# Attention by straight and cross halves in a chain of linear attention and two feed-forward layers

## Chip, cores and metric

One core of one Trainium2 chip runs the whole program. The time is device microseconds from launch to end, as the median of three runs, and lower is better.

## The reference, cut to what matters

Attention is a decayed linear recurrence: for each of 4 batches and 8 heads a 64x64 state is multiplied by the head's decay and takes the outer product of k and v at each of 768 positions, and q reads it. Two feed-forward layers follow (512 to 1024 to 512 with a softmax gate and a layer norm, then 512 to 2048 to 512 with h cos h).

```python
gamma = 1.0 - 2.0 ** (-5.0 - np.arange(H))
for t in range(S):
    state = gamma[None, :, None, None] * state + np.einsum('bhd,bhe->bhde', k[:, :, t], v[:, :, t])
    y[:, :, t] = scale * np.einsum('bhd,bhde->bhe', q[:, :, t], state)
```

```python
h = x @ w_in
e = np.exp(h - np.max(h, axis=-1, keepdims=True))
solu = h * e / (np.sum(e, axis=-1, keepdims=True) + 1e-09)
ln = (solu - mu) / np.sqrt(var + 1e-06) * g_ln
x = ln @ w_out          # second layer: (h * np.cos(h)) @ w_out
```

The weights arrive as 64-bit floats and are turned into 32-bit ones on the chip.

## The kernel before, in words

**Attention steps.** The sequence is cut into 12 chunks of 64 positions; two batches go together, so there are 24 steps (`steps`, line 80), and a step holds 8 heads of two batches: 16 blocks of 64x64. A partition half of 64 rows holds the even heads, the other the odd ones; `j` counts the 8 column blocks. A step n has three batches of matmuls. *Scores* (`score_pair`, line 225): q times k of the chunk, into the PSUM tile `sc`; the operands lie in the other half from the output, so they use the cross corners of the array. *State* (`state_pair`, line 233): k times v of the chunk, accumulated over the chunks into the PSUM tile `S`, in the straight corners. *Outputs* (`att_out`, line 282): one matmul per block over all 128 rows. For that, tile `W` holds v in one half and the state before the chunk in the other, and tile `X` holds the masked scores in the one half and q in the other, so that one product of 128 rows adds both contributions, into the PSUM tile `y`.

**Around the matmuls.** `score_mask` (line 244) is two products on VectorE of 64 partitions each, by a table `mg` of mask and decay that GpSimd scales for each step (`att_prep`, line 216). `att_prep` also scales k by its decay, in four ScalarE operations (line 223). `state_copy` (line 253) is two ScalarE copies of 64 partitions, which move the state to the other half. The output product with the second part of `mg` (line 290) makes `x32`, the rows that the first layer takes. `load_step` (line 83) issues six loads per step on SP's queue: kt, q in two halves, v in two halves, kn; a step's tiles are reused three steps later (`kt`: two).

**Order.** TensorE's order is the program's, written out by hand. The other engines' queues are filled by a planner that simulates a timeline, so an operation can be queued there ahead of its place in the program. Each engine's queue runs in its order. Lines 489 to 518 write out the first steps; from then on `attend` (line 457) is called between the pieces of the first layer: up to line 533 once per half block of rows, then in the loop from line 537 once or twice per round. While weights are still read two at a time (before line 536) scores, state and outputs are three batches; after it scores of step n+1 and state of step n alternate, and the outputs of step n follow.

**What else runs there.** `load_w` (line 142) turns a weight tile into 32-bit floats in one ScalarE operation and four VectorE operations (lines 158 to 168). `norm` (line 318) is the softmax gate and layer norm of 128 rows, with a power on GpSimd (line 334), whose result VectorE (335) and ScalarE (336) wait for. `transp` (line 341) transposes the result, 16 transposes into a PSUM tile that ScalarE and VectorE (line 355) empty. After some 350 us only the second layer is left.

Of the kernel before, what the change touches and what calls it, by code (L numbers as in the profile page):

```python
# [22 lines left out]
C = 64  # L23
# [27 lines left out]
def body(ctx: ExitStack, tc: tile.TileContext, qx, kt, kn, vn, c_sc, c_mg,  # L51
# [31 lines left out]
    def load_step(n):  # L83
        bp, i = steps[n]
        d = {}
        d["kt"] = pa.tile([128, 8, C], F32, tag="kt", name="kt", bufs=2)
        d["X"] = pa.tile([128, 2, 8, C], F32, tag="X", name="X")
        d["kn"] = pa.tile([128, NHP, 2 * D], F32, tag="kn", name="kn")
        d["W"] = pa.tile([128, 2, 8, D], F32, tag="W", name="W")
        d["mg"] = pa.tile([128, 2, NHP, C], F32, tag="mg", name="mg", bufs=2)  # L90
        nc.sync.dma_start(out=d["kt"], in_=kt[bp, i].rearrange("p (j s) -> p j s", s=C))
        src = qx[bp, i].rearrange("p (j s) -> p j s", s=C)
        nc.sync.dma_start(out=d["X"][64:128, 0], in_=src[64:128])
        nc.sync.dma_start(out=d["X"][0:64, 1], in_=src[0:64])
        src = vn[bp, i].rearrange("p (j s) -> p j s", s=D)
        nc.sync.dma_start(out=d["W"][0:64, 0], in_=src[0:64])
        nc.sync.dma_start(out=d["W"][64:128, 1], in_=src[64:128])
# [7 lines left out]
    mg = const.tile([128, 2, NHP, C], F32, name="mg")  # L105
    cs = const.tile([128, 3, NI, NHP], F32, name="cs")
    gcol = const.tile([128, K1], F32, name="gcol")
    nc.scalar.dma_start(out=mg, in_=c_mg.rearrange("p (u a t) -> p u a t", u=2, t=C))
    nc.scalar.dma_start(out=cs, in_=c_sc.rearrange("p (u a t) -> p u a t", u=3, t=NHP))
# [106 lines left out]
    def att_prep(n):  # L216
        bp, i = steps[n]
        d = st[n]
        nc.gpsimd.tensor_tensor(out=d["mg"], in0=mg, in1=cs[:, 0:2, i].unsqueeze(3).to_broadcast([128, 2, NHP, C]),
                                op=ALU.mult)  # L220
        if i + 1 < NI:
            for a in range(NHP):
                nc.scalar.activation(out=d["kn"][:, a], in_=d["kn"][:, a], func=AF.Copy, scale=cs[:, 2, i, a:a + 1])  # L223

    def score_pair(n, j):
        d = st[n]
        if j == 0:
            d["sc"] = psa.tile([128, 8, C], F32, tag="sc", name="sc")
        sc = d["sc"]
        nc.tensor.matmul(out=sc[0:64, j], lhsT=d["kt"][64:128, j], rhs=d["X"][64:128, 0, j], start=True, stop=True)  # L230
        nc.tensor.matmul(out=sc[64:128, j], lhsT=d["kt"][0:64, j], rhs=d["X"][0:64, 1, j], start=True, stop=True)

    def state_pair(n, j):
# [4 lines left out]
        sp = s_ps[0]  # L238
        k3 = d["kn"].rearrange("p a (b d) -> p (a b) d", b=2)
        for r, par in ((slice(0, 64), 0), (slice(64, 128), 1)):  # L240
            nc.tensor.matmul(out=sp[r, j], lhsT=k3[r, j], rhs=d["W"][r, par, j],
                             start=(i == 0 and j == 0), stop=(i == NI - 2 and j == 7), skip_group_check=True)

    def score_mask(n):
        d = st[n]
        sc = d["sc"]
        for r, par in ((slice(0, 64), 0), (slice(64, 128), 1)):
            nc.vector.tensor_tensor(  # L248
                out=d["X"][r, par].rearrange("p (a b) t -> p a b t", b=2),
                in0=sc[r].rearrange("p (a b) t -> p a b t", b=2),  # L250
                in1=d["mg"][r, 0].unsqueeze(2).to_broadcast([64, NHP, 2, C]), op=ALU.mult)

    def state_copy(n):
        nd, sp = st[n + 1], s_ps[0]
        nc.scalar.activation(out=nd["W"][64:128, 0], in_=sp[0:64], func=AF.Copy)
        nc.scalar.activation(out=nd["W"][0:64, 1], in_=sp[64:128], func=AF.Copy)

    def att_scores(n):
        for j in range(8):
            score_pair(n, j)  # L260
        score_mask(n)

    def att_state(n):
        if steps[n][1] + 1 >= NI:
            return
        for j in range(8):
            state_pair(n, j)
        state_copy(n)

    def att_both(n):  # L270
        if steps[n][1] + 1 >= NI:
            att_scores(n + 1)
            return
        for j in range(8):
            score_pair(n + 1, j)
            state_pair(n, j)
        score_mask(n + 1)
        state_copy(n)
# [3 lines left out]
    def att_out(n):  # L282
        d = st[n]
        y = psa.tile([128, 8, C], F32, tag="y", name="y")
        for j in range(8):
            for par in range(2):
                nc.tensor.matmul(out=y[64 * par:64 * par + 64, j], lhsT=d["W"][:, par, j], rhs=d["X"][:, par, j],  # L287
                                 start=True, stop=True)
# [378 lines left out]
```

## Time and profile before

| | before |
|---|---|
| median of 3 runs | 932.8 us (928.63 to 934.05) |
| profiled execution, first to last instruction | 932.8 us |
| TensorE busy | 893.4 us |
| VectorE busy | 622.7 us |
| ScalarE busy | 455.5 us |
| GpSimd busy | 48.0 us |
| granted TensorE clock, mean | 0.985 |

In the profile, PE is TensorE and PEld its weight loads, DVE is VectorE, ACT ScalarE, POOL GpSimd and SP the queue that issues DMAs; a q behind an engine's name is its sequencer. An engine's busy time counts the time in which at least one of its operations runs. PEclk is the granted share of TensorE's full clock. An fp32 matmul is recorded as two passes, so a batch of 16 has 32 records.

### The profile page before, as it was taken

How to read it: one execution, taken by the hardware profiler on the slowest of the kernel's cores; microseconds unless marked ns; L12 is line 12 of the kernel's file. 1: busy time of each engine (PE TensorE's matmuls, PEld its weight loads, DVE VectorE, ACT ScalarE, POOL GpSimd, SP SyncE). 2: the span in 40 equal slices, each digit the busy share in tenths (PEclk: the TensorE clock that was granted, in tenths of full speed). 3: DMA queues.
4: the chain of work that ended last, by engine and by line, in shares of the span. 5: the costliest groups of instructions: out<-in, count | busy, mean ns of one | idle time of the engine just before them, and what ended most of it. 6: DMA issues, size and time to landing. Idle time of an engine off the chain costs nothing.

```text
span 932.8 us, 16044 instructions
## 1 busy us (share of the span) xinstructions
PE 893.4 (96%) x6464; PEld 765.1 (82%) x6464; DVE 622.7 (67%) x1090; ACT 455.5 (49%) x768; POOL 48.0 (5%) x60
## 2 busy tenths in 40 slices
PE   4787999989899999999999999999999999999997
PEld 4676889879799989998888888888888888888886
DVE  6899887587667754566766655756575665656654
ACT  4677666556656555554534333433443343344332
POOL 2112100101011000000000000000000000000000
PEclk7999899989999999999999999999999999999999
DMA  9986354565547422133012002000300030001001
GB/s 260 313 252 194 106 158 146 184 204 161 188 131 226 157 93 90 64 108 111 24 35 56 1 1 73 19 0 1 91 1 1 7 84 1 1 24 45 1 1 46
DMA packets 41884, 85.28 MB, mean 91 GB/s; under 512 B 5457, under 2 KB 11729, under 8 KB 41809
## 3 DMA queue, kind: packets, MB, share of 16 engines
q1 hardware_dynamic: 41376, 83.91, 30.0%
q8 instruction: 51, 0.84, 0.4%
q10 hardware_dynamic: 432, 0.34, 0.1%
q14 instruction: 25, 0.20, 0.1%
HBM read 64.30 MB, written 19.92 MB: 90 GB/s over the span
## 4 chain that ended last, share of the span: by engine, by line
PE 84%; DVE 6%; DMA 5%; ACT 2%; issue 2%; SPq 1%; POOL 0%; DVEq 0%; ACTq 0%
PE h L393 28%; PE acc L418 28%; PE y L368 13%; PE h L315 10%; DMA kn<-kn_dram 3%; PE tr L351 2%; PE y L287 2%; DMA W<-vn_dram 1%; PE sc L230 1%; DVE X L248 1%; DVE wt L164 1%; DVE wt L161 1%; ACT kn L223 1%; ACT junk L328 1%; DVE wt L162 0%
## 5 line engine op out<-in xcount | busy, mean ns | idle before, releaser
L393 PE MATMUL h<-yh,w2h 128*128 128x512 f32 x384 | 149.6, 390 | 0.0
L393 PE MATMUL h<-yl,w2h 128*128 128x512 f32 x384 | 149.4, 389 | 0.0
L393 PE MATMUL h<-yh,w2l 128*128 128x512 f32 x384 | 149.4, 389 | 0.0
L418 PE MATMUL acc<-o2h,gh 128*128 128x512 f32 x384 | 149.4, 389 | 0.0
L418 PE MATMUL acc<-o2h,gl 128*128 128x512 f32 x384 | 149.4, 389 | 0.0
L418 PE MATMUL acc<-o2l,gh 128*128 128x512 f32 x384 | 149.4, 389 | 0.0
L404 ACT ACTIVATE r<-r,hp 128x512 f32<-128x512 f32 x96 | 69.5, 724 | 144.5 <-DVE r L403 144.5
L368 PE MATMUL y<-lth,o1h 128*128 128x256 f32 x384 | 110.2, 287 | 0.0
L368 PE MATMUL y<-ltl,o1h 128*128 128x256 f32 x384 | 108.8, 283 | 0.0
L368 PE MATMUL y<-lth,o1l 128*128 128x256 f32 x384 | 108.6, 283 | 0.0
L401 DVE SCALAR_TENSOR_TENSOR r<-ki,h 128x512 f32<-128x512 int32 x96 | 66.0, 687 | 62.9 <-ACT ki L400 61.9
L405 DVE TENSOR_TENSOR r<-r,h 128x512 f32<-128x512 f32 x96 | 66.0, 687 | 61.6 <-ACT r L404 61.6
L128 DVE TENSOR_TENSOR gl<-r,gh 128x512 fp32r<-128x512 f32 x96 | 66.3, 691 | 45.9 <-ACT gh L125 45.4
L400 ACT ACTIVATE ki<-h 128x512 int32<-128x512 f32 x96 | 57.3, 597 | 74.7 <-PE h L393 74.1
L125 ACT ACTIVATE gh<-r 128x512 fp32r<-128x512 f32 x96 | 60.7, 632 | 65.4 <-DVE r L405 65.4
L393 PEld LDWEIGHTS h<-yh,w2h 128*128 128x128 f32 x384 | 72.1, 188 | 14.9
L418 PEld LDWEIGHTS acc<-o2h,gl 128*128 128x128 f32 x384 | 72.1, 188 | 15.0
L393 PEld LDWEIGHTS h<-yl,w2h 128*128 128x128 f32 x384 | 72.1, 188 | 15.0
L418 PEld LDWEIGHTS acc<-o2l,gh 128*128 128x128 f32 x384 | 72.1, 188 | 14.9
L418 PEld LDWEIGHTS acc<-o2h,gh 128*128 128x128 f32 x384 | 72.0, 188 | 14.9
L393 PEld LDWEIGHTS h<-yh,w2l 128*128 128x128 f32 x384 | 72.1, 188 | 14.8
L315 PE MATMUL h<-w1h,xh 128*128 128x512 f32 x192 | 77.9, 406 | 0.0
(77 smaller groups left out, 1554.3 us busy)
## 6 DMA issues: line engine op xcount, KB each, us to landing
raw<-w_in_dram SPq DMA_DIRECT2D x24, 512.0 KB, 4.4
raw<-w_out_dram SPq DMA_DIRECT2D x24, 512.0 KB, 4.8
kt<-kt_dram SPq DMA_DIRECT2D x24, 256.0 KB, 4.9
X<-qx_dram SPq DMA_DIRECT2D x48, 128.0 KB, 5.0
W<-vn_dram SPq DMA_DIRECT2D x48, 128.0 KB, 4.6
kn<-kn_dram SPq DMA_DIRECT2D x24, 256.0 KB, 5.1
y1d<-ys SPq DMA_DIRECT2D x24, 256.0 KB, 2.1
yt<-y1d SPq DMA_DIRECT2D x24, 256.0 KB, 2.9
```

What stands on the lines that cost most here:

```text
L125: op = nc.scalar.activation(out=hi, in_=src if head is None else head, func=AF.Copy)
L128: nc.vector.tensor_tensor(out=lo, in0=src, in1=hi.bitcast(F32), op=ALU.subtract)
L287: nc.tensor.matmul(out=y[64 * par:64 * par + 64, j], lhsT=d["W"][:, par, j], rhs=d["X"][:, par, j], start=True, stop=True)
L315: nc.tensor.matmul(out=h[:, c], lhsT=a[:, k], rhs=w[:, k, cs], start=(k + m == 0), stop=(k == KD - 1 and m == 2))
L351: nc.tensor.transpose(out=tr[:, e, t * 128:(t + 1) * 128], in_=lns[2 * g + t].rearrange("p c f -> p (c f)")[:, j * 128:(j + 1) * 128], ide ...
L368: nc.tensor.matmul(out=y1[:, e], lhsT=w[:, j, ds], rhs=a[:, j % 2], start=(m == 0), stop=(m == 3 * K1 - 1))
L393: nc.tensor.matmul(out=h, lhsT=w[:, k, cs], rhs=a[:, k], start=(m == 0), stop=(m == 3 * KD - 1))
L400: nc.scalar.activation(out=ki, in_=h, func=AF.Identity, scale=INV2PI, bias=0.25)
L401: nc.vector.scalar_tensor_tensor(out=r, in0=ki, scalar=-C1, in1=h, op0=ALU.mult, op1=ALU.add)
L404: nc.scalar.activation(out=r, in_=r, func=AF.Sin, bias=hp[:, 0:1])
L405: nc.vector.tensor_tensor(out=r, in0=r, in1=h, op=ALU.mult)
L418: nc.tensor.matmul(out=acc, lhsT=a[:, ts_], rhs=w, start=(j == 0 and m == 0), stop=(j == K2 - 1 and m == 2))
```

## The change

Each head stays on one half of the rows. Scores and state are products within a half (the straight corners). The output is no longer one product of 128 rows but two of 64, masked scores times v (`intra`) and state times q, both into the opposite half of `y` (the cross corners), accumulated there. Since scores, state and outputs of a pair of blocks then occupy different corners, `attn` alternates all of them: first scores of step n+1 with the intra products of step n, then state of step n with the state products of step n. v is scaled by its decay instead of k, by GpSimd in place; the mask is a plain triangle from a constant table, applied by one VectorE operation over 128 partitions; the state copy is one ScalarE operation into a tile of its own. k, q, v and k again are laid side by side in DRAM, and a step is loaded by two DMAs of 512 KB. The rows of the first layer's weight are swapped on the host to fit the swapped halves.

```diff
-        nc.sync.dma_start(out=d["kt"], in_=kt[bp, i].rearrange("p (j s) -> p j s", s=C))
-        ...
-        nc.sync.dma_start(out=d["kn"], in_=kn[bp, i].rearrange("p (j s) -> p j s", s=2 * D))
-        if i == 0:
-            nc.gpsimd.memset(d["W"][64:128, 0], 0.0)
-            nc.gpsimd.memset(d["W"][0:64, 1], 0.0)
+        t = pa.tile([128, 4, 8, C], F32, tag="kqvk", name="kqvk")
+        d["kt"], d["q"], d["v"], d["kn"] = (t[:, u] for u in range(4))
+        src = kqvk[bp, i].rearrange("p (u j s) -> p u j s", u=4, s=C)
+        nc.sync.dma_start(out=t[:, 0:2], in_=src[:, 0:2])
+        nc.sync.dma_start(out=t[:, 2:4], in_=src[:, 2:4])
+        d["g"] = pa.tile([128, NHP, C], F32, tag="g", name="g", bufs=2)
+        d["M"] = pa.tile([128, 8, C], F32, tag="M", name="M", bufs=2)
 ...
     def att_prep(n):
-        nc.gpsimd.tensor_tensor(out=d["mg"], in0=mg, in1=cs[:, 0:2, i].unsqueeze(3).to_broadcast([128, 2, NHP, C]),
+        v = d["v"].rearrange("p (a b) e -> p a (b e)", b=2)
+        nc.gpsimd.tensor_tensor(out=v, in0=v, in1=cs[:, 1, i].unsqueeze(2).to_broadcast([128, NHP, 2 * D]), op=ALU.mult)
+        nc.gpsimd.tensor_tensor(out=d["g"], in0=mg[:, 1:], in1=cs[:, 0, i].unsqueeze(2).to_broadcast([128, NHP, C]),
                                 op=ALU.mult)
-        if i + 1 < NI:
-            for a in range(NHP):
-                nc.scalar.activation(out=d["kn"][:, a], in_=d["kn"][:, a], func=AF.Copy, scale=cs[:, 2, i, a:a + 1])
 ...
+    half = (slice(0, 64), slice(64, 128))
     def score_pair(n, j):
+        for r in half:
+            nc.tensor.matmul(out=d["sc"][r, j], lhsT=d["kt"][r, j], rhs=d["q"][r, j], start=True, stop=True)
 ...
+    def out_pair(n, intra, j):
+        l, r = (d["v"], d["M"]) if intra else (d["s"], d["q"])
+        for p in range(2):
+            nc.tensor.matmul(out=d["y"][half[1 - p], j], lhsT=l[half[p], j], rhs=r[half[p], j],
+                             start=(intra and j == 0), stop=(j == 7 and (not intra or steps[n][1] == 0)),
+                             skip_group_check=True)
 ...
     def score_mask(n):
+        nc.vector.tensor_tensor(out=d["M"], in0=d["sc"], in1=mg[:, 0].unsqueeze(1).to_broadcast([128, 8, C]), op=ALU.mult)
     def state_copy(n):
+        s = pa.tile([128, 8, D], F32, tag="s", name="s", bufs=2)
+        nc.scalar.activation(out=s, in_=s_ps[0], func=AF.Copy)
 ...
+    def attn(scores=None, state=None, outs=None):
+        one, two = [], []
+        if scores is not None:
+            one += [(score_pair, scores, j) for j in range(8)]
+        if state is not None and steps[state][1] + 1 < NI:
+            one += [(state_pair, state, j) for j in range(8)]
+        if outs is not None:
+            two += [(out_pair, outs, intra, j) for intra in ((True, False) if steps[outs][1] else (True,)) for j in range(8)]
+        for k in range(max(len(one), len(two))):
+            for q in (one, two):
+                if k < len(q):
+                    q[k][0](*q[k][1:])
+                    if q[k][0] is score_pair and q[k][2] == 7:
+                        score_mask(scores)
 ...
     def attend():
-        if n == 0:
-            att_state(n)
-            att_out(n)
         if n + 1 < ns:
             att_prep(n + 1)
-            if n > 0 and "lt" in p2:
-                att_both(n)
-            else:
-                att_scores(n + 1)
-        if n > 0:
-            if "lt" not in p2:
-                att_state(n)
-            att_out(n)
+        attn(n + 1 if n + 1 < ns else None, n, n)
```

The hand-written first steps (lines 489 to 518) call `attn` for the same batches in the same places.

## Rows read from the trace of the kernel before

**Rows 1.** The page's first part: busy us, share of the span, instructions.

```profile
PE 893.4 (96%) x6464; PEld 765.1 (82%) x6464; DVE 622.7 (67%) x1090; ACT 455.5 (49%) x768; POOL 48.0 (5%) x60
```

**Rows 2.** Stretches: busy us of PE, PEld, DVE, ACT, POOL; PEclk, DMA share, GB/s.

```profile
0.00:27.00 27.00, 14.92 (x231) 13.18 (x232) 14.94 (x26) 13.06 (x27) 5.14 (x13) 0.81 0.96 282
27.00:95.00 68.00, 53.17 (x878) 44.29 (x877) 66.15 (x118) 50.36 (x102) 14.11 (x14) 0.96 0.84 239
95.00:420.00 325.00, 317.30 (x3118) 287.32 (x3118) 224.78 (x438) 189.93 (x315) 28.79 (x34) 0.98 0.46 144
```

**Rows 3.** VectorE's timeline, 23 to 42 us: start us, us, instruction, idle before.

```profile
26.63 0.69 DVE L128 TENSOR_TENSOR w1l<-raw,w1h 128x512 fp32r<-128x512 f32 x1 [2.98 <-ACT w1h L125]
...
38.47 0.69 DVE L290 TENSOR_TENSOR x<-y,mg 128x512 f32<-128x512 f32 x1
39.08 0.68 DVE L167 SCALAR_TENSOR_TENSOR raw<-raw,wt 128x512 int32<-128x512 int32 x1
39.68 1.38 DVE L248 TENSOR_TENSOR X<-sc,mg 64x512 f32<-64x512 f32 x2
41.09 0.69 DVE L167 SCALAR_TENSOR_TENSOR raw<-raw,wt 128x512 int32<-128x512 int32 x1
```

**Rows 4.** VectorE by line, 27 to 95 us: busy us, mean ns, idle.

```profile
L248 DVE TENSOR_TENSOR X<-sc,mg 64x512 f32<-64x512 f32 x18 | 12.3, 684 | 0.2
L167 DVE SCALAR_TENSOR_TENSOR raw<-raw,wt 128x512 int32<-128x512 int32 x11 | 10.1, 919 | 0.1
...
L161 DVE TENSOR_SCALAR wt<-wt 128x512 f32<-128x512 f32 x11 | 6.2, 572 | 0.0
```

**Rows 5.** GpSimd by line, 0 to 420 us.

```profile
L219 POOL TENSOR_TENSOR mg<-mg,cs 128x512 f32<-128x512 f32 x24 | 27.2, 1137 | 210.1 <-DVE x L290 162.0 <-DVE sm L330 45.2 <-DMA cs<-c_sc_dram 2.4
```

**Rows 6.** Three lines of VectorE over the run: duration ns min/median/max.

```profile
L161 DVE TENSOR_SCALAR wt<-wt x48: 414/421/1269, 10.2 to 329.9; 128x512 f32<-128x512 f32 x48
...
L164 DVE SCALAR_TENSOR_TENSOR wt<-raw,wt x48: 674/691/694, 11.1 to 333.0; 128x512 int32<-128x512 int32 x48
...
L167 DVE SCALAR_TENSOR_TENSOR raw<-raw,wt x16: 681/690/1534, 12.1 to 97.1; 128x512 int32<-128x512 int32 x16
```

**Rows 7.** Waits of the run; TensorE's after 93 us: us, times, longest.

```profile
ACT kn L223 <- DMA kn<-kn_dram: 36.0, 16, 5.7
...
PE tr L351 <- DVE ltl L355: 7.6, 5, 4.1
```

**Rows 8.** Two more stretches of the span, columns as in rows 2.

```profile
15.00:20.00 5.00, 2.41 (x32) 2.06 (x32) 5.00 (x9) 1.60 (x4) 1.35 (x1) 0.50 1.06 226
45.00:50.00 5.00, 4.37 (x138) 3.99 (x131) 4.96 (x13) 3.98 (x7) 0.32 (x1) 1.00 1.04 397
```

**Rows 9.** Timeline of TensorE over one attention step in the steady stage.

```profile
220.08 0.22 PE L230 MATMUL sc<-X,kt 64*64 64x64 f32 x1
220.08 0.22 PE L231 MATMUL sc<-X,kt 64*64 64x64 f32 x1
220.09 0.23 PE L241 MATMUL S<-W,kn 64*64 64x64 f32 x2
...
220.89 0.22 PE L230 MATMUL sc<-X,kt 64*64 64x64 f32 x1
...
221.06 1.15 PE L287 MATMUL y<-X,W 128*64 128x64 f32 x32
222.14 0.39 PE L368 MATMUL y<-lth,o1h 128*128 128x256 f32 x1
```

**Rows 10.** The chain of waits, 171 to 192 us: start us, us, what.

```profile
173.33 7.86 DMA kn<-kn_dram
...
181.22 1.28 ACT kn L223 x4
...
183.90 0.56 POOL sm L334
```

**Rows 11.** Landing of the W transfer issued at 175.64 us.

```profile
DMA to landing us min/median/max: 6.7/6.7/6.7
```

More of the change, by code (lines that the diff above doesn't have):

```diff
@@ L50, in body @@
 @with_exitstack
-def body(ctx: ExitStack, tc: tile.TileContext, qx, kt, kn, vn, c_sc, c_mg,
+def body(ctx: ExitStack, tc: tile.TileContext, kqvk, c_sc, c_mg,
          w_in1, w_out1, gln, w_in2, w_out2, out):
@@ L237, in state_pair @@
             s_ps[0] = psa.tile([128, 8, D], F32, tag="S", name="S")
[L238 to L241, printed above, removed]
+        for r in half:
+            nc.tensor.matmul(out=s_ps[0][r, j], lhsT=d["kn"][r, j], rhs=d["v"][r, j],
                              start=(i == 0 and j == 0), stop=(i == NI - 2 and j == 7), skip_group_check=True)
+    def out_pair(n, intra, j):
+        d = st[n]
+        if j == 0 and intra:
+            d["y"] = psa.tile([128, 8, C], F32, tag="y", name="y")
+        l, r = (d["v"], d["M"]) if intra else (d["s"], d["q"])
[3 more added lines that the diff above has]
+                             skip_group_check=True)
@@ new lines, in state_copy @@
+    def state_copy(n):
+        s = pa.tile([128, 8, D], F32, tag="s", name="s", bufs=2)
+        st[n + 1]["s"] = s
+        nc.scalar.activation(out=s, in_=s_ps[0], func=AF.Copy)
[13 more added lines that the diff above has]
+                        score_mask(scores)
+        if state is not None and steps[state][1] + 1 < NI:
+            state_copy(state)
+        if outs is not None:
+            att_out(outs)
@@ L283, in att_out @@
         d = st[n]
[L284 to L288, printed above, removed]
+        y = d["y"]
         x32 = moe.tile([128, NHP, 128], F32, tag="x32", name="x32", bufs=RING)
@@ L495, in body @@
     att_prep(0)
-    att_scores(0)
+    attn(scores=0)
     weights(KD)
-    att_state(0)
-    att_out(0)
+    attn(state=0, outs=0)
     att_prep(1)
-    att_scores(1)
+    attn(scores=1)
     split_x(0)
-    att_state(1)
-    att_out(1)
+    attn(state=1, outs=1)
     mm1(0, 0, [0, 1])
     att_prep(2)
-    att_scores(2)
+    attn(scores=2)
     load_step(3)
@@ L510, in body @@
     mm1(0, 0, [2])
-    att_state(2)
+    attn(state=2)
     mm1(0, 0, [3])
-    att_out(2)
+    attn(outs=2)
     att_prep(3)
-    att_scores(3)
+    attn(scores=3)
     nxt[0] = 3
@@ L612, in _consts @@
     hp = np.arange(NHP)
-    head = 2 * hp[None, :] + (p[:, None] >= 64)
-    gh = gam[head]
-    sl = (p % 64)[:, None, None]
-    mask = np.where(t[None, None, :] >= sl, gh[:, :, None] ** (-1.0 * sl), 0.0)
-    kf = gh[:, None, :] ** (-(64.0 * i[None, :, None] + sl - S / 2))
-    g = gh[:, :, None] ** t[None, None, :] / math.sqrt(D)
-    at = (gh[None] ** (64.0 * i[:, None, None] - S / 2))[..., None]
-    at = at[..., 0]
-    mg = np.stack([mask, g], axis=1).reshape(128, 2 * NHP * C)
-    cs = np.stack([1.0 / at, at, kf.transpose(1, 0, 2)]).transpose(2, 0, 1, 3).reshape(128, 3 * NI * NHP)
+    sl = p % 64
+    par = p // 64
+    gs, gy = (gam[2 * hp[None, :] + m[:, None]] for m in (par, 1 - par))
+    tri = np.where(t[None, :] >= sl[:, None], 1.0, 0.0)[:, None]
+    kf = gs[:, None, :] ** (-(64.0 * i[None, :, None] + sl[:, None, None] - S / 2))
+    g = gy[:, :, None] ** t[None, None, :] / math.sqrt(D)
+    at = gy[:, None, :] ** (64.0 * i[None, :, None] - S / 2)
+    mg = np.concatenate([tri, g], axis=1).reshape(128, (1 + NHP) * C)
+    cs = np.stack([at, kf], axis=1).reshape(128, 2 * NI * NHP)
     return [np.ascontiguousarray(a.astype(np.float32)) for a in (cs, mg)]
```

68 lines of the change are left out of this document (12 added, 56 removed).

## The prediction

> **What bounds the kernel now.** I read the shares first: TensorE is busy nearly the whole span and VectorE two thirds of it [rows 1], but this is an average over stages, so next came the busy times by stretch [rows 2]. The reader is to see three stages there. From 27 to 95 us VectorE is busy 66.15 of 68 us while TensorE has 15 us to spare: VectorE is the bound. From 95 to 420 us TensorE is busy 317.3 of 325 us. After 420 us no attention is left and the change touches nothing. Before 27 us the DMA engines are busy 96% and everything waits for loads. So the first 95 us are to be costed by VectorE and DMA, the stretch from 95 to 350 us by TensorE's own columns and its few waits.
>
> **VectorE: the mask.** Each attention step has two mask products of 64 partitions (lines 248). The timeline shows the slots: the pair that starts at 39.68 lets the next operation start at 41.09, so it takes 1.41 us, and one 128-partition product out of PSUM (L290) takes 39.08 - 38.47 = 0.61 us [rows 3]. The new mask is one operation of that shape: 0.80 us less per step. In the VectorE-bound stage 18 such products stand, nine pairs [rows 4]: 9 x 0.80 = 7.2 us. VectorE hardly idles there, so I count all of it on the path. The floor is 4.0 us, five pairs, if only those after 50 us count because loads hold the others.
>
> **GpSimd: v and g.** Before, GpSimd multiplies 128x512 once per step, 1.137 us [rows 5]. After, it multiplies v (128x512, the same size, so 1.14) and g (half as many columns; by proportion 0.57): 0.57 us more per step, 5.1 us over nine steps. This costs VectorE something. In the same stretch L161 and L167 average 572 and 919 ns [rows 4] where their medians over the run are 421 and 690 [rows 6]: 11 x (151 + 229) = 4.2 us of lengthening, with GpSimd busy 14.11 us [rows 2]. That is 0.30 us per us of GpSimd, so 5.1 us more give 1.5; other operations are lengthened too, so I take 2. Bounds: 0, if the new operations fall beside operations that are not lengthened, and 5.1, if VectorE stands for all of it.
> The Trainium skill, SBUF — State Buffer, "Who interferes with whom", says that a GpSimd operation and a VectorE one that needs their shared port pair exclude each other for a whole instruction, and lists among these VectorE operations with two inputs in SBUF. By that rule alone the 5.1 us would all be lost and the sum would be 3 us higher. The trace agrees only in part: L164 has two SBUF inputs and its longest of 48 is 694 ns against a median of 691 [rows 6].
>
> **ScalarE: four k products and one of two state copies leave.** ScalarE is busy 50.36 of 68 us [rows 2], so its own time costs nothing. What its in-order queue holds up does. Before 26.63 us VectorE stands idle for 2.98 us until ScalarE's w1h arrives [rows 3], and ScalarE waited 36.0 us in 16 places for the DMA of kn [rows 7], one of these just ahead of that w1h. With kn untouched by ScalarE this wait is gone; what is late next is the raw weight's DMA. I take 2.5 of the 2.98 us; bounds 0 and 4, the upper with the loads' gain below.
>
> **DMA.** Six transfers per step (kt, two of X, two of W, kn; rows of 2 KB, four of them on 64 partitions) become two of 512 KB with rows of 4 KB, the form of a raw weight load. Bytes are the same. Where only attention loads land the chip moved 226 GB/s; in a stretch with raw loads, 397 [rows 8]. 1 MB at these rates is 4.6 and 2.6 us, so two steps early in the queue could come 4 us sooner. I don't add this to the 2.5 us, since what VectorE waits for is the ordered work ahead of w1h; it is why I expect no load to take the place of the kn wait. SP issues four transfers fewer per step. Both halves now wait for the end of step n-3's output products, where kt and kn were free earlier by one batch of matmuls.
>
> **TensorE.** Before, a step in the steady stage is 16 groups of four matmuls, one in each quadrant of the array, 0.058 us apart ((220.89 - 220.08) / 14), then 16 pairs of 128-row matmuls from 221.06 to 222.14, 1.08 us [rows 9]. I take 1.09 us for the first batch, the same 16 spacings with a start, so both are 2.17 us. After, 16 straight pairs and 16 cross pairs alternate, in two passes each: 32 groups of four. At the same spacing and one start of 0.16 us (1.08 - 16 x 0.058) that is 2.02 us. Fourteen steps run after 95 us. Twelve save 0.15 us, the one at the end of a batch pair saves as much or nothing, and the last, which has outputs only, goes from 1.08 to 2.0: together about -0.9 us. In the early stage three separate batches become one, but TensorE has room there and I count nothing.
>
> **Waits in the TensorE stage.** The transposes wait 7.6 us in five places for VectorE's ltl [rows 7]. The chain through the longest shows why: kn's DMA of 173.33 lands at 181.2, ScalarE's kn at 181.22 stood in front of the square (junk), so the power on GpSimd came only at 183.90 [rows 10]. The clock, 0.98 on the mean of that stage, is worth at most 325 x 0.02 = 6.5 us more [rows 2]. After the change the square no longer stands behind a DMA, but the power may: GpSimd's product of v waits for the second load of its step. In the trace W, which carries v, lands at 175.64 + 6.7 = 182.3 [rows 11], 1.1 us after kn; with 1.14 and 0.57 us behind it the power could start at 184.0, no gain. If the power stands ahead of v in GpSimd's queue, all is gained. I take 4 us between 0 and 14.
>
> **Sum.** -7.2 + 2 - 2.5 - 0.9 - 4 = -12.6 us. The profiled execution's span is 932.8 us and the median of the timed runs is 932.8 too, so nothing has to be converted: 920 us.
>
> **Rivals.**
> *The loads hold the first stage and the queue is no better* (little gain): four masks are hidden behind loads that land when they did, no start gain, no wait gained: -4.0 + 1 - 0.9 = -3.9, 929 us. For it: DMA busy 0.96 up to 27 us. Against: VectorE has no gap over 27 to 95 us but 1.85 us.
> *All head-of-line waits go* (more gain): v's product stands behind the power everywhere and the larger rows land early: -7.2 + 2 - 4 - 0.9 - 12 = -22, 911 us.
> *GpSimd takes ScalarE's place and does worse* (slower): the product of v is queued ahead of the power, so the power, VectorE's L335 behind it, ScalarE's L336 behind that and in the end ltl wait for the later half of the load. It decides from the point where v lands more than about 1 us after kn did, because kn's and the square's 2.4 us leave the chain and 1.7 us come in. Ten loads are issued after 95 us; at 2 us lost in each, half the longest wait of 4.1 [rows 7], TensorE loses 20 us against early gains of 8.6: 944 us. Against it: ltl made TensorE wait in five places only, though ScalarE waited in 16.
> *The cross pairs do not run beside the straight ones* (slower): 64 pairs of 0.058 make 3.7 us per step, +1.55 x 14 = 22 us, less 8.6 and 4: 942 us. Against it: the four-quadrant groups of L230, L231 and L241 [rows 9] are the same four tiles, with score and state where score and output will be.
> The Trainium skill, TensorEngine Tiling (Array Packing), "Gotcha 1: PSUM Pressure", says that different row tiles cannot use one PSUM bank at once; by it the two cross outputs in bank y would follow each other, the case just priced. The rows speak against it: L230 and L231 read different rows, write one bank and both start at 220.08 [rows 9].
>
> **How the numbers follow.** Forecast (916 to 926) 0.50; little gain 0.20; more gain 0.18; GpSimd 0.08; cross pairs 0.04. The likeliest is 920. Range: from 908, the more-gain case with 3 us for its clock, to 931, past the little-gain case; the slower cases are left out. Within 0.5% (928.1 to 937.5) is what a measurement here cannot tell from no change: about two thirds of the little-gain case and a little of the slower ones, 0.15. Faster takes the forecast, the more-gain case and the rest, 0.75; slower 0.10.
>
> **What would show it.** Right: VectorE's mask as 24 products of 128x512 near 0.69 us; the stretch in which VectorE has no gaps ends some 8 us sooner, near 87 instead of 95 us; the attention batch near 2.0 us; no ScalarE wait on a load of kn. Wrong: GpSimd waiting on the kqvk load with VectorE's L335 behind it and TensorE idle before transposes more than before; a batch of 3 us or more; L161, L162 and L167 lengthened beyond 1 us each on the mean. If that stretch ends near 95 us again, the case of the loads holds.

## The result: slower, 942 us against 931

The changed kernel takes 941.57 us (median of four runs, 938.61 to 942.76) beside 930.71 for the kernel before in the same runs (927.43 to 934.05): ratio 1.011, 95% interval 1.0077 to 1.0144. The forecast of 920, its range to 931 and the 0.75 for faster all miss.

The first part of its profile answers to [rows 1], the stretches to [rows 2]; the last stretch is shown for both kernels, since the rows ahead of the prediction stop at 420 us.

```profile
span 940.2 us, 17197 instructions
PE 898.7 (96%) x7168; PEld 762.4 (81%) x7168; DVE 608.0 (65%) x1066; ACT 413.9 (44%) x658; POOL 63.1 (7%) x80
```

The changed kernel by stretch (columns as in [rows 2]):

```profile
0.00:27.00 27.00, 12.32 (x263) 11.11 (x264) 18.49 (x33) 11.28 (x18) 9.12 (x14) 1.00 0.94 367
27.00:95.00 68.00, 48.26 (x1103) 40.53 (x1104) 53.71 (x95) 29.38 (x46) 18.60 (x19) 0.85 0.54 184
95.00:420.00 325.00, 322.74 (x3577) 292.20 (x3577) 220.23 (x432) 171.80 (x270) 35.33 (x47) 0.99 0.48 152
420.00:925.00 505.00, 505.00 (x2184) 410.43 (x2183) 310.68 (x501) 198.51 (x319) 0.00 (x0) 1.00 0.09 25
```

The last stretch of the kernel before:

```profile
420.00:925.00 505.00, 505.00 (x2230) 418.15 (x2229) 315.51 (x508) 201.06 (x323) 0.00 (x0) 1.00 0.10 27
```

The busy times of VectorE and ScalarE and the rate of the loads moved as forecast: VectorE from 66.15 down to 53.71 us in the second stretch, ScalarE from 50.36 to 29.38, and the loads from 282 up to 367 GB/s in the first. But TensorE's busy time in the second stretch fell too, from 53.17 to 48.26 us, and its granted clock from 0.96 to 0.85: it waits more and arrives later. In the last stretch it is busy throughout in both kernels at full clock, and gets through 2184 instead of 2230 matmul records.

To see where the time goes, one matmul is followed through the traces, by the start in us: the 97th of the first layer's first product, the first of its second product (this ends the first stage), the first of the second layer's second product (`acc`), and the last of all. Matmuls come in the same order in all kernels but for the attention's own, so a difference between two columns is what the stretch between them cost.

| kernel | 97th of first layer | first of second product | first `acc` | last `acc` |
|---|---|---|---|---|
| before | 86.6 | 103.0 | 416.5 | 927.6 |
| changed | 96.8 | 108.9 | 413.2 | 935.0 |
| changed, filler tile gone (e1) | 96.5 | 105.9 | 412.8 | 924.0 |
| e1, three batches early (f1) | 92.4 | 108.0 | 413.1 | 924.3 |
| e1, outputs apart everywhere (f2) | 90.9 | 107.2 | 427.5 | 938.7 |
| e1, v scaled on ScalarE (f3) | 100.3 | 115.7 | 427.4 | 938.5 |
| e1, mask in two products (j1) | 100.6 | 111.6 | 423.7 | 934.9 |
| e1, second y tile (h1) | 93.3 | 105.6 | 412.5 | 923.7 |
| f1, second y tile, g behind v (h13) | 88.9 | 105.0 | 412.1 | 923.4 |
| e1, weight pieces later (i1) | 96.8 | 107.9 | 413.2 | 924.4 |
| f1, second y tile, pieces later (i3) | 89.9 | 106.1 | 412.1 | 923.3 |
| e1, second y tile, state half first (k1) | 88.2 | 104.1 | 409.7 | 920.9 |

The changed kernel is 5.9 us late at the end of the first stage (the prediction had 7.7 early: -7.2 + 2 - 2.5), gains 9.2 us to the first `acc` (4.9 predicted) and loses 10.6 us from there to the end, in code that nobody touched. 5.9 - 9.2 + 10.6 = 7.3, and the two spans differ by 7.4, 940.2 - 932.8.

Each row of the table is one execution, and executions of one kernel scatter by some microseconds. The one of the kernel before is a long one: its span is 932.8 us, where the 13 runs of that kernel beside e1 have spans of 927.1 to 930.5 and a median of 929.1. f1's row is long too, 929.6 against a median of 927.4. So up to 3.7 us of a distance to the first row and some 2 us of one to f1's can belong to those executions; no trace says in which stretch. Against a usual execution of the kernel before, the 5.9 us can be up to 9.6 or the 9.2 as little as 5.5, and what the changed kernel gains up to the first `acc`, 3.3 us here, is about nothing. That fits the medians, which are 10.9 us apart, about the loss behind the first `acc`. The forecast starts from 932.8 too, 2 us above the 930.7 of four runs.

### The profile page after: what moved, and what is told of

The parts are those of the page before. It is cut to its first block, busy times and chain, and to the rows that moved or that the text cites. A ratio compares the mean times of both kernels' runs of the same rounds, so it can differ in the third digit from the quotient of the medians.

```text
span 940.2 us, 17197 instructions
## 1 busy us (share of the span) xinstructions
PE 898.7 (96%) x7168; PEld 762.4 (81%) x7168; DVE 608.0 (65%) x1066; ACT 413.9 (44%) x658; POOL 63.1 (7%) x80
## 4 chain that ended last, share of the span: by engine, by line
PE 83%; DVE 10%; issue 2%; ACT 2%; DMA 1%; POOL 0%; SPq 0%; DVEq 0%; ACTq 0%
PE h L380 28%; PE acc L405 28%; PE y L355 12%; PE h L302 9%; PE tr L338 2%; DVE wt L155 2%; PE y L239 1%; DVE wt L152 1%; PE sc L222 1%; DVE wt L153 1%; DVE raw L158 1%; DVE u L312 1%; DVE sm L310 1%; PE S L230 1%; DMA raw<-w_in_dram 1%
## 5 line engine op out<-in xcount | busy, mean ns | idle before, releaser
L405 PE MATMUL acc<-o2h,gl 128*128 128x512 f32 x384 | 151.4, 394 | 0.0
L405 PE MATMUL acc<-o2h,gh 128*128 128x512 f32 x384 | 151.4, 394 | 0.0
L380 PE MATMUL h<-yh,w2l 128*128 128x512 f32 x384 | 151.4, 394 | 0.0
L380 PE MATMUL h<-yl,w2h 128*128 128x512 f32 x384 | 151.3, 394 | 0.0
L355 PE MATMUL y<-ltl,o1h 128*128 128x256 f32 x384 | 108.9, 284 | 0.0
L380 PEld LDWEIGHTS h<-yl,w2h 128*128 128x128 f32 x384 | 72.1, 188 | 16.8
L405 PEld LDWEIGHTS acc<-o2h,gl 128*128 128x128 f32 x384 | 72.4, 188 | 16.2
```

The source lines that it names most:

```text
L355: nc.tensor.matmul(out=y1[:, e], lhsT=w[:, j, ds], rhs=a[:, j % 2], start=(m == 0), stop=(m == 3 * K1 - 1))
L380: nc.tensor.matmul(out=h, lhsT=w[:, k, cs], rhs=a[:, k], start=(m == 0), stop=(m == 3 * KD - 1))
L405: nc.tensor.matmul(out=acc, lhsT=a[:, ts_], rhs=w, start=(j == 0 and m == 0), stop=(j == K2 - 1 and m == 2))
```

## Experiments

**The second layer: a tile that shrank.** The changed kernel's constant tables are 960 bytes smaller (`mg` 768, `cs` 192), so every tile behind them on the left side of SBUF lies 960 bytes lower: the weights `w1h`, later `w2h`, and the halves of `o2`. Those allocated from the right side (`w2h0`, `yh`, `gh`) did not move. 960 is 64 less than 1024, so the distance between the two sides changed by 64 bytes modulo 512. No trace prints an address: the shifts follow from the sizes in the kernels' text, and the kernel before counts as 0 here, as a multiple of 512 in the expectations below. The trace of the changed kernel has matmuls of both kinds. First the second layer's first product while both operands are on the right, then one with the weight on the left and the input on the right, then `acc`:

```profile
496.61 0.39 PE L380 MATMUL h<-yh,w2l 128*128 128x512 f32 x1
...
501.60 0.39 PE L380 MATMUL h<-yl,w2h 128*128 128x512 f32 x1
...
599.74 0.39 PE L380 MATMUL h<-yh,w2h 128*128 128x512 f32 x1
...
601.61 0.39 PE L380 MATMUL h<-yl,w2h 128*128 128x512 f32 x1
601.84 0.40 PE L405 MATMUL acc<-o2h,gh 128*128 128x512 f32 x1
...
602.77 0.40 PE L405 MATMUL acc<-o2h,gl 128*128 128x512 f32 x1
```

The same two kinds in the kernel before, both with one operand on each side:

```profile
599.63 0.39 PE L393 MATMUL h<-yh,w2l 128*128 128x512 f32 x1
...
601.22 0.39 PE L393 MATMUL h<-yl,w2h 128*128 128x512 f32 x1
601.44 0.39 PE L418 MATMUL acc<-o2h,gh 128*128 128x512 f32 x1
...
602.58 0.39 PE L418 MATMUL acc<-o2l,gh 128*128 128x512 f32 x1
```

Start to start: (501.60 - 496.61) / 22 = 0.227 us with both on one side, then (601.61 - 599.74) / 8 = 0.234 and (602.77 - 601.84) / 4 = 0.232, against 0.227 and 0.228 before ((601.22 - 599.63) / 7, (602.58 - 601.44) / 5). Over the whole stretch the mean is 233.3 ns for the 864 first products with one operand on each side and 230.9 for the 1152 of `acc`, 226.7 for both before: 5.7 + 4.8 = 10.5 of the 10.6 us. TensorE does not wait; the matmul itself is slower. Five kernels move only these addresses, by the size of the filler tile `pad` or of `hp`, the first tile on the right:

```diff
-    const.tile([128, 16], F32, name="pad")                        # e1: gone; e3: [128, 32]; e5: [128, 64], ahead of all constants
-    hp = p_hp.tile([128, 120], F32, name="hp")                    # e2: [128, 104]
+    hp = p_hp.tile([128, 104], F32, name="hp")
```

In e4 the filler tile goes from the kernel before.

Filler tile gone (e1): 

> The changed kernel without the 64-byte tile named pad, so that every tile on the left side of SBUF (weights of both layers, o2) starts at a multiple of 512 bytes again, as in the kernel before; nothing else differs. In the profile of the changed kernel the second layer's matmuls are 231 to 233 ns apart where an operand lies on the left and the other on the right, against 227 before. Theory 'placement': all of them return to 227 ns, the second layer takes 10.6 us less, the time is about 931 us (941.6 - 10.6), level with before. Rival 'the pace comes from elsewhere' (more instructions, clock): pace stays at 232 ns, 941 us.

Right side shifted too (e2): 

> The changed kernel, with the first tile on the right side of SBUF 64 bytes shorter, so that the tiles of the right side also start 64 bytes past a multiple of 512, as those of the left do. Theory 'the offset between the two operands of a matmul': both operands lie alike again, all second-layer matmuls are 227 ns apart, 931 us. Rival 'an operand must itself start at a multiple of 128 or 512 bytes': the pace stays 232 ns and the first quarter of the up products, both of whose operands lie on the right and which ran at 227 ns, slows to 233 too, 943 us.

Filler of 128 bytes (e3): 

> The changed kernel with the tile named pad of 128 bytes instead of 64: the left side starts 128 bytes past a multiple of 512, the right side at a multiple. If 64-byte offsets alone are bad and 128 is enough, 227 ns and about 931 us; if the operands must agree to 256 or 512 bytes, 232 ns and about 941 us.

Kernel before without filler (e4): 

> The kernel before without its 64-byte tile named pad: its left side then starts 448 bytes past a multiple of 512, 64 past a multiple of 128; nothing of the change is in it. Theory 'placement': the second layer's mixed matmuls slow to 231 to 233 ns, about 10 us more, 941 us. Rival 'it belongs to the new attention': 227 ns, 931 us.

Filler of 256 bytes (e5): 

> The changed kernel with a filler tile of 256 bytes in place of 64, which puts the left side's operands 256 bytes past a multiple of 512, the right side's stay at a multiple. If only the multiple of 512 counts: the second layer's matmuls that take one operand from each side at 231 to 234 ns, the time near 941 to 945. If half of it is as good: 227 ns everywhere and 931.

| kernel | left side, shift in bytes modulo 512 | right side | first product, `acc`, ns | time, us |
|---|---|---|---|---|
| before | 0 | 0 | 226.7, 226.7 | 930.9 |
| changed | 64 | 0 | 233.3, 230.9 | 941.6 |
| e1 | 0 | 0 | 226.7, 226.7 | 931.24 |
| e2 | 64 | 64 | 226.7, 226.7 | 933.2 (one run) |
| e3 | 128 | 0 | 233.1, 233.1 | 944.7 (one run) |
| e4 | 448 | 0 | 231.4, 233.3 | 947.7 (one run) |
| e5 | 256 | 0 | 226.7, 226.7 | 932.1 (one run) |

e1 stands at 1.0001 of the kernel before (0.9991 to 1.0011): the filler tile alone is worth 10.3 us. e2 decides what counts: both sides shifted by 64 bytes are as good as none, so it is not an operand's own place but the distance between the two. Of the distances tried, 0 and 256 cost nothing and 64, 128 and 448 cost 2 to 3%. e4 puts the same kind of loss into the old kernel, 11.8 us from the first `acc` on. e2 to e5 ran once each; their verdict rests on the pace of the 2016 matmuls in each trace. What in the chip makes the distance matter, no run shows, nor why the two kinds of product differ. e1 is the base of all that follows but j2.

**The first stage: is VectorE's time worth anything?** The prediction's largest term rests on it. e1 still comes 2.9 us late to the end of this stage, or more against a usual execution of the kernel before. j1 gives the saved mask time back, j2 takes the same from the kernel before.

```diff
+        for r in half:                                            # j1
+            nc.vector.tensor_tensor(out=d["M"][r], in0=d["sc"][r], ...)
+            if par:                                               # j2, in the kernel before
+                nc.scalar.activation(out=d["X"][r, par], in_=sc[r], func=AF.Copy)
+                continue
```

> Base: the changed kernel without its filler tile (931.2 us), with the mask again as two VectorE products of 64 partitions per step, which gives back the 0.8 us a step that the change saved. Theory A (VectorE's throughput sets the first stage, as the prediction had it): nine steps of 0.75 us, the 97th first-layer matmul 5 to 7 us later than 96.5 and the end 936 to 938. Rival B (VectorE has some 13 us to spare there and only the order and the waits count): the 97th matmul within 2 us of 96.5, the end 930 to 933.

> The kernel before, with one of a step's two mask products taken from VectorE and replaced by a plain copy on ScalarE, so that half of the scores is left unmasked and undecayed. It takes 0.7 us a step from VectorE and changes nothing else. Theory A (in the kernel before VectorE sets the first stage, 66 of 68 us busy): nine steps of 0.7 us, the first product of the second matrix 4 to 6 us before 102.95 and the end at 925 to 927. Rival B (TensorE, the loads and the serial norm chain hold the stage as well): no more than 2 us sooner there, the end 929 to 931, or later if the copies stand behind ScalarE's wait for k.

j1: 942.25 us, 1.0123 (1.0086 to 1.016). The stage ends 5.7 us later than in e1, and another 5.2 us go after it, where TensorE's waits for `ltl` grow from 2.8 to 6.6 us. After 95 us, in e1 and then in j1 (us, times, longest):

```profile
PE tr L337 <- DVE ltl L341: 2.8, 4, 1.0
PE tr L338 <- DVE ltl L342: 6.6, 4, 3.2
```

So the mask's saving was real. That is theory A in kind, but its figures missed: the 97th came 4.1 us later, not 5 to 7, and the end lies beyond 938. VectorE is busy only 54.58 of 68 us in e1, and yet the longer mask costs TensorE time. Whether it does so by what it holds up in VectorE's queue or because TensorE waits for the mask itself, j1 does not separate. The granted clock from 37 to 92 us is lower too, 0.83 against 0.88.

j2: 942.9 us, 1.0132 (1.0098 to 1.0167), 5.9 us later at the end of the stage. It does not weigh VectorE's time: ScalarE took the copies in, and TensorE waited for them (5 waits for ScalarE's X up to 95 us, 12.2 us). This is rival B's last clause: three of the copies stood behind ScalarE's products of k, which had waited for their loads. The last of the three, on ScalarE:

```profile
44.95 1.28 ACT L223 ACTIVATE kn<-kn,cs 128x128 f32<-128x128 f32 x4 [4.10 <-DMA kn<-kn_dram]
46.26 0.60 ACT L249 ACTIVATE X<-sc 64x512 f32<-64x512 f32 x1
```

So work that is added to ScalarE's queue in the kernel before comes late behind these waits. How near the path that queue was without it, j2 does not show.

**v on ScalarE instead of GpSimd (f3).**

```diff
-        nc.gpsimd.tensor_tensor(out=v, in0=v, in1=cs[:, 1, i].unsqueeze(2).to_broadcast(...), op=ALU.mult)
+        for a in range(NHP):
+            nc.scalar.activation(out=v[:, a], in_=v[:, a], func=AF.Copy, scale=cs[:, 1, i, a:a + 1])
```

> v is scaled by four ScalarE operations per step instead of one GpSimd operation; all batches merged. Theory 'GpSimd': the state products of steps 0 and 1 waited 2.1 and 5.3 us for GpSimd's v, whose queue stood behind g, and GpSimd's g took 3.7 us there instead of 0.6 beside a dense VectorE; without v the first layer starts 4 to 6 us sooner and VectorE's operations are less lengthened: 924 to 928 us. Theory 'merged batch': the waits at 48 to 96 us stay as they are, the early gain is eaten by them: 929 to 932 us.

945.46 us, 1.0178 (1.0154 to 1.0202). In f3 ScalarE waits for the load again, and TensorE waits before the transposes, which answers to both lines of [rows 7]. ScalarE's waits up to 420 us, then TensorE's after 95:

```profile
ACT kqvk L211 <- DMA kqvk<-kqvk_dram: 21.9, 9, 7.7
PE tr L338 <- DVE ltl L342: 10.0, 5, 3.7
```

The changed kernel after 95 us, where GpSimd takes the wait for the load:

```profile
POOL kqvk L211 <- DMA kqvk<-kqvk_dram: 22.9, 10, 4.5
PE tr L338 <- DVE ltl L342: 1.0, 2, 0.8
```

Keeping this wait off ScalarE is worth 14.5 us in the new kernel, 9.8 of them in the first stage; the prediction allowed 2.5 and 4 for the old one. The two are not quite the same move: before, ScalarE scaled k, which only the state products read, and v, which f3 puts there, is read by the output products too.

**What then takes the first stage's time back? Is it the output batch?** f1 puts scores, state and outputs apart there, as the kernel before had them; f2 puts the outputs apart everywhere.

```diff
-        attn(n + 1 if n + 1 < ns else None, n, n)
+        if "lt" in p2:                                            # f2: outputs apart here too
+            attn(n + 1 if n + 1 < ns else None, n, n)
+        else:
+            attn(scores=n + 1)
+            attn(state=n)
+            attn(outs=n)
```

> From here on every kernel is the changed one without the 64-byte pad (931.2 us). This one issues scores, state and outputs as three batches in this order, as the kernel before did, in the calls up to line 533; later steps stay merged. Theory 'merged batch': the output products of step n stand right behind the first score pair, so TensorE's queue stops there until VectorE has emptied y of step n-1 (and written M of n), and with it the scores, the state and the first layer behind them; in the profile TensorE stands idle 17 us between 43 and 97 us, against 10 before. Undone, the first piece of the first layer that came at 96.5 us comes 5 to 8 us sooner and the time is 924 to 927 us. Rival 'GpSimd': the waits are for v, which GpSimd scales, so the order of TensorE's work does not matter: 930 to 932 us.

> As the run before it, and in the later steps too the outputs follow scores and state as a batch of their own (scores and state alternate, as in the kernel before). Theory 'the later merging is worth one start per step': a step's attention takes about 2.2 us instead of 2.02, fourteen steps, so 1.5 to 2.5 us more than the run with only the early batches apart. Rival 'the merged batch waits in the late stage as well': faster than it.

f1: 929.19 us, 0.9989 (0.9972 to 1.0007). Its 97th matmul came 4.1 us sooner than in e1, short of the 5 to 8 expected, and the end of the stage no sooner. f2: 945.71, 1.0176 (1.0157 to 1.0194). TensorE from 27 to 95 us, output products only, first before, then in f1 (columns as in [rows 5]):

```profile
L287 PE MATMUL y<-X,W 128*64 128x64 f32 x256 | 10.5, 237 | 5.6 <-DVE X L248 4.9 <-DVE x L290 0.5
```

```profile
L238 PE MATMUL y<-M,kqvk 64*64 64x64 f32 x256 | 10.8, 244 | 7.7 <-DVE M L244 4.9 <-DVE x L276 2.8
L238 PE MATMUL y<-kqvk,s 64*64 64x64 f32 x256 | 10.4, 241 | 0.0
```

Apart, an output takes two products of 64 rows where one of 128 did, and TensorE is busy with them 21.2 us instead of 10.5. f1 becomes TensorE-bound by that: 52.16 of 55 us from 37 to 92. Later on, f2 shows what merging is worth for outputs in this form: a step takes 3.7 us (221.96 to 225.67) instead of 2.0, and some 14 us are lost by the end, where 1.5 to 2.5 were expected. Merged, as in the change, the products cost nothing extra in the steady stage (a step of 2.02 us, below), but each group stands in one order with three others, and TensorE waits for whichever is late. Its waits in e1, 27 to 95 us (us, times, longest):

```profile
PE y L238 <- POOL sm L320: 6.6, 2, 4.1
PE y L238 <- DVE M L244: 5.0, 1, 5.0
PE sc L221 <- DVE sm L313: 2.6, 1, 2.6
PE y L238 <- issue: 1.9, 2, 1.6
PE sc L221 <- DVE M L244: 1.6, 2, 1.1
```

These are 17.7 us. Where a line of the norm (sm) is named, VectorE's x or M stood behind the norm's short operations. The clock fell with them: from 37 to 92 us it was 0.88 in e1, where the kernel before has 0.99. What the lower clock itself cost is not separated from the waits.

**Which of the waits is it?** Five small edits, each on e1 unless said otherwise.

```diff
+        d["g"] = pa.tile([128, NHP, C], F32, tag="g", name="g", bufs=3)                 # f4 (2)
+            pool = p2["psb"] if n % 2 and "pst" not in p2 else psa                      # h1: second y tile
+            d["y"] = pool.tile([128, 8, C], F32, tag="y", name="y")
+        tc.keep_in_program_order(nc.gpsimd.tensor_tensor(out=d["g"], ...))              # h3: g just ahead of x
-        if seq[0] > 2 * KD:                                                             # i1: weight pieces
+        if seq[0] > KD:
```

Three g tiles (f4): 

> The g tile has three buffers instead of two, so GpSimd's g of step n+2 no longer waits until VectorE has used g of step n, and the v product queued behind it does not either; all batches merged, v on GpSimd. If the queue order on GpSimd is what costs, TensorE's 5.3 us wait at 15.3 us goes to under 2 us, and 3 to 4 us remain at the end: 927 to 929 us. If GpSimd is held by VectorE's use of SBUF rather than by its queue, v still ends near 20 us and nothing changes: 930 to 932 us.

932.35 us, 1.0025 (1.001 to 1.0041). The g of step 1 still ran from 16.2 us for 3.73 us, and nothing moved.

Second y tile (h1): 

> Base: the changed kernel without its 64-byte filler tile (931.2 us). In the first stage the outputs of odd steps go into a second PSUM tile, so that the output batch of step n need not wait until VectorE has read those of step n-1; after it one tile as before. Theory A (in the merged batch scores and state of the next step stand behind an output product that waits for the one y tile; TensorE waits there 6.6 us in two places between 27 and 95 us behind the norm's small operations on VectorE): these waits go, the 97th first-layer matmul comes at about 90 instead of 96.5 us and the end 3 to 4 us sooner, 927 to 928. Rival B (what the outputs wait for is VectorE's in-order queue as a whole; the next wait, for the masked scores, takes the place of this one): the 97th matmul within 1.5 us of 96.5 and the end within 1 us of 931.

930.76 us, 1.0003 (0.9987 to 1.0018). The 97th matmul came 3.2 us sooner, half of what theory A had, the end of the stage 0.3 us: theory A in part as far as the 97th, rival B at the end.

g behind v (h3): 

> Base: the changed kernel without its filler tile (931.2 us). GpSimd's product g of a step is issued behind v's product, just ahead of its use, so that v(1) follows v(0) at about 10 us instead of standing behind a g that ran from 15.8 to 19.5. Theory A (GpSimd's queue holds the first state batches): TensorE's wait of 5.2 us at 15.3 goes down to about 1 us, the 49th first-layer matmul comes 2 to 4 us before 61.4, and the end 0 to 3 us sooner, 928 to 931. Rival B (the first matmuls of the first layer wait for weights that are ready at 24 us anyway, and g is then late for the x of its step on VectorE): the 49th matmul within 1 us of 61.4 and the end 931 to 933.

933.38 us, 1.0024 (1.0005 to 1.0043). The g of step 1 took 1.06 us instead of 3.73, but TensorE's wait at 16 us stayed 5.1 us long, now for the mask: GpSimd was not what it waited for last, and the stage ended 2.7 us later.

Weight pieces later (i1, and i2 on h1): 

> Base: the changed kernel without its filler tile (931.2 us). The four weight pieces for the second half of the first layer's columns may no longer be queued ahead of their place in the program; on VectorE's queue this puts x of step 1 ahead of all four and the mask of step 2 behind two of them, where both stood behind three or four. Theory A (the first stage comes late because VectorE's in-order queue works on these pieces, ready by 34.7 us and first used at 43, while TensorE waits 5.0 us for the mask of step 2): TensorE's wait at 30.7 goes to 1 to 2 us, the 25th first-layer matmul comes 1 to 3 us before 43.1, the 97th 2 to 4 us before 96.5, and the end at 927 to 930. Rival B (the pieces are then late in their turn, or the norm's chain sets the pace from 45 us on whatever comes before): the wait at 30.7 shrinks, but the 97th matmul lies within 1.5 us of 96.5 and the end within 1.5 us of 931.

> The same edit on the kernel with a second y tile in the first stage (930.8 us). Theory A: the two gains are in different places (the entry up to 43 us, the wait for y after 48 us), so the 97th matmul at 88 to 91 instead of 93.3 us and the end at 925 to 928. Rival B (the first transposes give it back): first product of the second matrix no more than 1 us before 105.6, the end at 929.5 to 931.

931.78 us, 1.0002 (0.9984 to 1.002), and 931.51, 1.0009 (0.9991 to 1.0027). The wait at 30.7 us went entirely and the 25th matmul came at 36.2 instead of 43.1 us, 6.9 sooner; at 43.5 us TensorE then stood 5.8 us for the next mask, and the 49th came 2.0 later than in e1. Rival B.

f1 with second y tile and g behind v (h13), and with second y tile and later pieces (i3): 

> Base: the changed kernel without its filler tile, with scores, state and outputs as three batches in the first stage (929.2 us), and to it both other edits: the second y tile in the first stage and g behind v. Theory A (the three hold-ups are separate): the 97th first-layer matmul at 86 to 89 instead of 92.4 us, the end at 925 to 927. Rival B (what is gained ahead of 95 us is given back at the first transposes, where VectorE is late): the 97th matmul sooner, but the first product of the second matrix no more than 1 us before 108 and the end 928 to 930.

> The same edit on the kernel with a second y tile and with scores, state and outputs as three batches in the first stage. TensorE had no wait of over 1 us between 37 and 92 us in the kernel that had both of these, so an earlier entry should be kept in full: the 97th matmul at 86 to 88 us. Theory A: the end at 926 to 928. Rival B (given back at the first transposes): the end at 929 to 931.

930.67 us, 0.9997 (0.998 to 1.0013), and 930.38, 0.9993 (0.9975 to 1.0011). In h13 TensorE is busy 53.80 of 55 us from 37 to 92 and reaches the 97th matmul at 88.9, but the stage ends at 105.0, 0.9 before e1. It waits 3.5 us for the norm ahead of the first transposes, as the kernel before did (3.8). Against e1, what is gained early is mostly given back by then. Against f1, on which it is built, h13 keeps 2.9 of its 3.5 us at the end of the stage and 1.0 at the first `acc`, with f1's row a long one. Rival B's figure for the stage (no more than 1 us before 108) missed, and the end lies just past its 928 to 930.

The two halves of the output batch exchanged (k1, on h1):

```diff
-            two += [(out_pair, outs, intra, j) for intra in ((True, False) if steps[outs][1] else (True,)) ...]
+            two += [(out_pair, outs, intra, j) for intra in ((False, True) if steps[outs][1] else (True,)) ...]
```

> Base: the changed kernel without its filler tile and with the second y tile in the first stage (930.8 us). The two halves of an output batch change places: state times q first, masked scores times v second, so that the mask of a step has half a batch more time and the scores of the next step no longer stand behind a product that waits for it. Theory A (the merged batch stalls on the mask: TensorE waits 5.6 us for it at 30 us and 1 to 1.4 us in later steps): the 97th first-layer matmul 2 to 5 us before 93.3 and the end at 926 to 929. Rival B (the state's copy on ScalarE is then what it waits for, since it too comes from the batch before): the 97th matmul within 1.5 us of 93.3 and the end 930 to 932.

927.98 us, 0.9968 (0.9951 to 0.9985): faster than both kernels, by 0.3% of the one before and 1.4% of the changed one's median. State times q needs only the state's copy, so the mask has half a batch more; the 97th comes 5.1 us sooner than in h1, theory A, the stage ends 1.6 sooner and the whole 2.8. TensorE's waits in k1, 27 to 95 us:

```profile
PE y L240 <- ACT s L251: 6.2, 3, 2.9
PE sc L221 <- DVE M L246: 3.3, 2, 3.1
PE tr L339 <- DVE x L278: 3.1, 1, 3.1
PE y L240 <- DVE M L246: 2.2, 1, 2.2
PE sc L221 <- DMA kqvk<-kqvk_dram: 2.0, 1, 2.0
```

The state's copy (s) has come up as the rival said, and these still make 16.8 us; but TensorE is busy 50.56 us of that stretch, 2.8 more than in e1, and after 95 us it waits 1.9 us before transposes.

## Why the prediction was wrong

**"After 420 us no attention is left and the change touches nothing"**: this step, taken at 0, cost 10.6 us, and e1 takes nearly all of it back. The prediction treated the size of a constant table as nothing, where it moved an operand of 2016 matmuls. It is the step that turned no change into slower.

**"In the early stage three separate batches become one, but TensorE has room there and I count nothing"**: this is the second failure, and it goes with a first stage that came 5.9 us late (2.9 in e1) instead of 7.7 early. Room on the mean was not room in the order: merged, the batch waited 17.7 us from 27 to 95 in e1; apart, the doubled output products filled the room (f1, 10.7 us), and the order of the halves inside the batch (k1) moved the stage's end by 1.6 us. That the batch is the cause is argued from these and not shown: no run isolates it, since the old output form doesn't fit the new tiles. Open stays what holds the first transposes: every variant of e1 that came over 3 us sooner than it to the 97th matmul (f1, f2, h1, h13, i3, k1) had lost over three quarters of that lead at the first of the second product.

**VectorE's mask, -7.2**: right in kind. M takes 0.68 to 0.69 us in all 24, and j1 measures 5.7 us for the stage and 10.9 in all. The reading "VectorE is the bound", though, was too simple: work put into ScalarE's queue, behind its waits for loads, delays the stage as much, in the kernel before (j2, 5.9 us) and in the new one (f3, 9.8).

**GpSimd, +2**: half of the 24 g took at most 0.62 us, near the 0.57 set for them, but one took 3.73, at 15.8 us. The two long ones, 3.73 and 3.40, lie beside dense VectorE work. The operations that [rows 6] had as never lengthened were lengthened here: L155, the L164 of before, took over 1400 ns in six places, up to 1456 against 694, each time within 0.4 us of the start of a v on GpSimd. The longest g, and the longest L155 with the v ahead of it:

```profile
15.82 3.73 POOL L212 TENSOR_TENSOR g<-mg,cs 128x256 f32<-128x256 f32 x1 [6.24 <-DVE x L277]
255.88 1.04 POOL L211 TENSOR_TENSOR kqvk<-kqvk,cs 128x512 f32<-128x512 f32 x1 [0.19 <-DMA kqvk<-kqvk_dram]
256.01 1.46 DVE L155 SCALAR_TENSOR_TENSOR wt<-raw,wt 128x512 int32<-128x512 int32 x1
```

The Trainium skill, SBUF — State Buffer, "Who interferes with whom", says that whoever issues first keeps the shared port pair for the whole instruction, whatever the shape; the trace agrees and has both engines losing, so the prediction's argument from L164 against this page was wrong. What it cost in all, no run prices: f4 and h3, which changed g's place and buffers, gained nothing.

**ScalarE and its wait for k, -2.5, and the waits in the TensorE stage, -4**: right in kind, too small. The wait for `ltl` fell from 7.6 to 1.0 us as the row foretold, and f3 prices the move, in the new kernel, at 14.5 us. The rival in which GpSimd takes ScalarE's place and does worse was wrong: GpSimd waits 22.9 us for loads after 95 us, and TensorE's waits before the transposes come to 1.0.

**TensorE's batch, -0.9**: right. In the steady stage the changed step starts at 218.68 and the next product at 220.70, 2.02 us as worked out:

```profile
218.68 0.28 PE L222 MATMUL sc<-kqvk 64*64 64x64 f32 x2
218.69 0.27 PE L239 MATMUL y<-M,kqvk 64*64 64x64 f32 x2
...
219.66 0.23 PE L230 MATMUL S<-kqvk 64*64 64x64 f32 x2
219.67 0.22 PE L239 MATMUL y<-kqvk,s 64*64 64x64 f32 x2
...
220.70 0.39 PE L355 MATMUL y<-lth,o1h 128*128 128x256 f32 x1
```

The cross pairs do run beside the straight ones, so the rival at 942 us, whose time came out, did so for another reason.

**The loads**: the rate was right, 367 GB/s up to 27 us. The 25th matmul of the first layer still came at 43.7 us instead of 41.2; no run isolates what the loads gave.

## What to carry to other kernels

When a tile changes size, look at where the tiles behind it come to lie: the distance between the two operands of a long run of matmuls is worth checking before any term of the change. An engine that is busy 97% of a stretch, with others at 74 and 78%, doesn't hold it alone; ask which queue stands ahead of each wait, and test it by giving the saved time back. Before batches are merged, list what each part waits for: merging makes all of them wait for the latest, and the order of the parts inside the batch decided here between no gain and 0.3%.

## What the runs showed of the hardware that was not expected

A 128x512 matmul after another took 226.7 ns at full clock when the distance of its two SBUF operands was that of the kernel before or 256 bytes off it modulo 512, and 231 to 233 ns when it was 64, 128 or 448 off. The Trainium skill, SBUF — State Buffer, "Who interferes with whom", has TensorE's two reads on ports of their own, waiting for nobody. By that the distance should make no difference; here it makes 2 to 3%, whatever it is that causes it. Loads with rows of 4 KB moved 367 GB/s up to 27 us where rows of 2 KB among them gave 282 in the same stretch. GpSimd's 128x256 product took 0.61 us at the shortest and 3.73 beside dense VectorE work.
